# Taking attention's keys in passes, with a banked start and tail: two transformer layers on one core

## The chip, the cores and the metric

The kernel runs on one core of a Trainium2 chip. The metric is the device time of one execution in microseconds (us), as the median of several. The core's engines run side by side and wait for each other by semaphores: TensorE (PE, matrix products into the eight banks of PSUM), VectorE (DVE), ScalarE (ACT, functions such as exp and tanh), GpSimd (POOL) and SyncE (SP, which starts transfers here). Each engine takes its own instructions in program order.

## The reference

Two identical rounds of an attention layer and a feed-forward layer (FFN) on x, 2048 rows of 512 numbers in bf16:

```python
x = x + _A_ref(_layernorm(x), A_wqkv, A_wo)     # attention, 32 heads of 16
x = x + _B_ref(_layernorm(x), B_w1, B_w2)       # FFN: silu(x @ w1) @ w2, w1 512x1792
x = x + _A_ref(_layernorm(x), A_wqkv, A_wo)     # the same weights again
x = x + _B_ref(_layernorm(x), B_w1, B_w2)

def _A_ref(x, wqkv, wo):
    qkv = (x @ wqkv).reshape(B, S, 3, H, Dh).transpose(2, 0, 3, 1, 4)
    q, k, v = qkv[0], qkv[1], qkv[2]
    scores = einsum("bhqd,bhkd->bhqk", q, k) * Dh ** -0.5
    p = softmax(scores)                          # over all 2048 keys
    o = einsum("bhqk,bhkd->bhqd", p, v)
    return o.transpose(0, 2, 1, 3).reshape(B, S, D) @ wo
```

With heads of only 16, the exponentials (2 x 32 x 2048 x 2048) weigh more than the products.

## The kernel before

Rows are taken in four chunks of 512 queries; L is the round (0 or 1), qc the chunk, g one of four groups of eight heads, par the half of a group (heads are packed four at a time, j, into rows of 32 with the other half masked to zero), kt one of 16 tiles of 128 keys. One *block* is the scores of one head against one key tile, 128 keys x 512 queries. All blocks of both rounds form one stream. A *step* takes three blocks (even steps) or two (odd steps) through one exp on ScalarE; on even steps one more block may take its exp on VectorE, in integer and fp16 arithmetic (`emit_d`, `step_d`).

```python
blocks = list(stream())          # for L, qc, g, par, kt (16), j (4)
while pos < len(blocks):
    n = 3 - len(steps) % 2
    a = blocks[pos : pos + n]                                       # ScalarE's
    pos += n
    d = blocks[pos : pos + 1] if n == 3 and pos % 64 < D_LAST else []   # VectorE's, D_LAST = 54
    pos += len(d)
    steps.append((a, d))
```

The rest of the work (layernorm, Q, K, V, output projection, FFN) is written as generators, and waits in a queue, `bg`. Each step of the stream lets the queue go one piece further (`pump`: two matmuls, or a layernorm part); a number yielded is a number of steps to rest. What the stream needs at once is forced (`ensure`), in one burst.

```python
for t, (a_blks, d_blks) in enumerate(steps):
    for L, qc, g, par, kt, j in a_blks + d_blks:
        ...
        if j == 0 and kt % 4 == 0:
            if kt == 0 and par == 0:
                bg.ensure(("q", L, qc, g))
            if qc == 0:
                c = kt // 4
                bg.ensure(("k", L, c, g))          # keys and values of chunk c of x
                bg.ensure(("v", L, c))
    s_ps = ps_s.tile([P, size, 512], FP32, ...)    # 3 banks or 2, one buffer each
    for i, blk in enumerate(a_blks):
        score(blk, s_ps[:, i, :])
    for blk in d_blks:
        emit_d(blk)
    ...                                            # P*V of steps t-3, t-2 on odd steps: emit_pv
    run_d()
    if not run_urgent(t):                          # a finished group's output: group_out
        bg.pump()
    p_tiles[t] = ppool.tile([P, size, 512], BF16, ...)
    nc.scalar.activation(p_tiles[t], s_ps, ACT.Exp, bias=shift, scale=SCALE)
# after the stream: the rest of the queue, one piece after the other
```

All background work shares one PSUM bank, `ps_m` (bufs=1). The two pieces that matter most:

```python
def layernorm_T(c, dst):
    ...                                            # bn_stats, bn_aggr of four tiles; rstd on GpSimd
    yield 2
    for i in range(4):
        xns.append(tensor_scalar(x_sb[:, 4 * c + i, :], mv, rstd))     # DVE, all four
    yield 0
    for i in range(0, 4, 2):
        t_ps = ps_m.tile(...)
        ...                                        # 8 transposes, then a DVE copy into dst

def ffn(L, c, emit):
    yield from layernorm_T(c, fT)
    for ft in range(FT):                           # 14
        h_ps = ps_m.tile(...)
        ...                                        # 4 matmuls
        nc.scalar.activation(t_sb, h_ps, ACT.Tanh, scale=0.5)
        nc.vector.scalar_tensor_tensor(hT[:, ft, :], t_sb, 1.0, h_ps, add, mult)
        yield 1
    for tq in range(4):
        y_ps = ps_m.tile(...)
        ...                                        # 14 matmuls, then x_sb += 0.5 * y_ps; round 1: store
```

`proj_v` begins with a GpSimd memset of its V tile. At a group's end `group_out` transposes the result (through `ps_m` too) and divides by the sum of the exponentials, which a column of ones in V brings along.

Of the kernel before, what the change touches and what calls it, by code (L numbers as in the profile page):

```python
# [10 lines left out]
ACT = mybir.ActivationFunctionType  # L11
# [7 lines left out]


class Background:

    def __init__(self):
        self.queue = deque()
        self.done = set()
        self.wait = 0
        self.inside = False

# [3 lines left out]
    def step(self):  # L32
        label, gen = self.queue[0]
        try:
            gap = next(gen)
            self.inside = gap is None
            return gap or 0
        except StopIteration:
            self.queue.popleft()
            self.done.add(label)  # L40
            return -1

    def pump(self):
        if self.wait > 0:
            self.wait -= 1
            return
        while self.queue:
            gap = self.step()
            if gap >= 0:
                self.wait = gap  # L50
                return
# [5 lines left out]
    def ensure(self, label):  # L57
        while label not in self.done:
            self.step()
            self.wait = 0  # L60
# [3 lines left out]
def kernel(  # L64
# [31 lines left out]
    D_LAST = 54  # L96
# [6 lines left out]
    qpool = ctx.enter_context(tc.tile_pool(name="qpool", bufs=6))  # L103
    xtpool = ctx.enter_context(tc.tile_pool(name="xtpool", bufs=4))
    ftpool = ctx.enter_context(tc.tile_pool(name="ftpool", bufs=1))
    xnpool = ctx.enter_context(tc.tile_pool(name="xnpool", bufs=4))
# [3 lines left out]
    apool = ctx.enter_context(tc.tile_pool(name="apool", bufs=2))  # L110
# [3 lines left out]
    ps_s = ctx.enter_context(tc.tile_pool(name="ps_s", bufs=1, space=bass.MemoryType.PSUM))  # L114
    ps_o = ctx.enter_context(tc.tile_pool(name="ps_o", bufs=1, space=bass.MemoryType.PSUM))
    ps_m = ctx.enter_context(tc.tile_pool(name="ps_m", bufs=1, space=bass.MemoryType.PSUM))
# [15 lines left out]
    x_sb = xpool.tile([P, NKT, D], BF16, name="x_sb")  # L132
    w_qkv = wpool.tile([P, CT, 3 * D], BF16, name="w_qkv")
    wo_sb = wpool.tile([P, CT, D], BF16, name="wo_sb")
    w1_sb = wpool.tile([P, CT, F], BF16, name="w1_sb")
    w2_sb = wpool.tile([P, FT, D], BF16, name="w2_sb")

    def load_x(c):
        nc.sync.dma_start(
            x_sb[:, 4 * c : 4 * c + 4, :],  # L140
            xf[512 * c : 512 * (c + 1), :].rearrange("(tt p) d -> p tt d", p=P),
        )

    load_x(0)
    nc.sync.dma_start(w_qkv[:], A_wqkv.rearrange("(ct p) f -> p ct f", p=P))
    for c in range(1, NC):
        load_x(c)
    nc.sync.dma_start(wo_sb[:], A_wo.rearrange("(ct p) e -> p ct e", p=P))
    nc.sync.dma_start(w1_sb[:], B_w1.rearrange("(ct p) f -> p ct f", p=P))
    nc.sync.dma_start(w2_sb[:], B_w2.rearrange("(ft p) e -> p ft e", p=P))  # L150

# [5 lines left out]
    attn = {}  # L157

    def layernorm_T(c, dst):
        mv = small.tile([P, 4, 2], FP32, name="mv", tag="mv")  # L160
        for i in range(4):
            st = small.tile([P, 6], FP32, name="st", tag="st")
            nc.vector.bn_stats(st[:], x_sb[:, 4 * c + i, :])  # L163
            nc.vector.bn_aggr(mv[:, i, :], st[:])
            if i == 1:
                yield 0
        rstd = small.tile([P, 4, 1], FP32, name="rstd", tag="rstd")
        nc.gpsimd.tensor_scalar_add(rstd[:], mv[:, :, 1:2], float(EPS))
        nc.gpsimd.tensor_tensor(out=rstd[:], in0=rstd[:], in1=half[:], op=ALU.pow)
        yield 2  # L170
        xns = []
        for i in range(4):
            xn = xnpool.tile([P, D], BF16, name="xn", tag="xn")
            nc.vector.tensor_scalar(  # L174
                out=xn[:],
                in0=x_sb[:, 4 * c + i, :],
                scalar1=mv[:, i, 0:1],
                scalar2=rstd[:, i, :],
                op0=ALU.subtract,
                op1=ALU.mult,  # L180
            )
            xns.append(xn)
        yield 0
        for i in range(0, 4, 2):
            t_ps = ps_m.tile([P, CT, 2, P], BF16, name="t_ps", tag="m")
            for u in range(2):
                for ct in range(CT):
                    nc.tensor.transpose(  # L188
                        t_ps[:, ct, u, :], xns[i + u][:, ct * P : (ct + 1) * P], ident[:, :]
                    )  # L190
                if u == 0:
                    yield None
            nc.vector.tensor_copy(
                out=dst[:, :, i * P : (i + 2) * P].rearrange("p c (u q) -> p c u q", u=2),
                in_=t_ps[:],
            )
            yield 0
# [4 lines left out]

    def proj_k(L, c, g):
        if g == 0:
            KT[L, c] = kpool.tile([P, NG, 512], BF16, name="KT", tag="KT")
        k_ps = ps_m.tile([P, 512], FP32, name="k_ps", tag="m")
        for ct in range(CT):
            nc.tensor.matmul(
                k_ps[:],
                lhsT=w_qkv[:, ct, D + P * g : D + P * (g + 1)],  # L210
                rhs=xnT[L, c][:, ct, :],
                start=(ct == 0),
# [441 lines left out]
```

The softmax here doesn't subtract the row's maximum and nothing guards it: scores larger than these inputs give would overflow.

## Time and profile before

| | us |
|---|---|
| median of 4 runs (2156.25 to 2164.57) | 2163.52 |
| span of the profiled execution | 2160.7 |
| ACT: exp of 3 blocks, 704 of them, mean of one | 1.591 |
| ACT: exp of 2 blocks, 704, mean of one | 1.167 |
| ACT: tanh of the FFN, 112, mean of one | 0.709 |
| DVE: first part of its exp (d_y), 576, mean of one | 0.687 |
| PE: scores (s_ps), 3520, mean of one | 0.423 |
| PE: second FFN matmul (f_ps), mean of one | 0.413 |

Lines of the profile name the engine, the source line, the operation and its tiles (out<-in), with shapes as partitions x elements. The means include overlap: the next instruction on an engine may start before the one ahead of it has ended. A square bracket at the end of a line of the timeline gives how long the engine was idle before it and what released it. In the row of slices each digit is the busy share of a fortieth of the span in tenths.

### The profile page before, as it was taken

What the parts mean: (1) busy time and instruction counts of PE and PEld (TensorE: products, weight loads), DVE (VectorE), ACT (ScalarE), POOL (GpSimd) and SP (SyncE); (2) the same over time, 40 slices, a digit from 0 to 9 for tenths busy, and PEclk for the clock granted to TensorE, in tenths of its full rate; (3) what the DMA queues carried; (4) which work ended last, traced back from release to release, by engine and by line L of the source; (5) the groups of instructions that cost most, each with busy time, mean ns of one, the idle gap of its engine ahead of it and who ended that gap; (6) DMA issues with size and microseconds to landing.
All of it is one profiled execution on the core that took longest, in us unless ns stands there. A gap on an engine that the chain in (4) does not pass through costs nothing.

```text
span 2160.7 us, 27606 instructions
## 1 busy us (share of the span) xinstructions
PE 1644.5 (76%) x10684; PEld 484.7 (22%) x10816; DVE 1468.6 (68%) x2923; ACT 1795.1 (83%) x1521; POOL 37.2 (2%) x47
## 2 busy tenths in 40 slices
PE   4687777787778887788657777778877787878756
PEld 1222112222222222222222222222222222222122
DVE  4577668768877787778524666767767776876641
ACT  1289999999999999989405999999998999999931
POOL 1100000000000000000000000000000000000000
PEclk9698779999999998999766787889988998999756
DMA  3000000000000000000000000000000000000000
GB/s 146 0 1 1 1 1 1 1 1 1 1 1 1 1 1 1 1 1 1 0 0 1 1 1 1 1 1 3 8 1 1 1 11 1 1 1 8 3 1 10
DMA packets 7939, 11.72 MB, mean 5 GB/s; under 512 B 384, under 2 KB 6784, under 8 KB 7808
## 3 DMA queue, kind: packets, MB, share of 16 engines
q1 hardware_dynamic: 7808, 9.96, 1.3%
q8 instruction: 84, 1.38, 0.3%
q14 instruction: 47, 0.39, 0.1%
HBM read 7.86 MB, written 2.10 MB: 5 GB/s over the span
## 4 chain that ended last, share of the span: by engine, by line
ACT 32%; PE 26%; issue 23%; DVE 18%; another core or an unknown queue 0%; POOL 0%; DMA 0%; ACTq 0%; POOLq 0%; DVEq 0%
ACT p_sb L603 29%; PE o_ps L434 8%; PE s_ps L526 6%; PE h_ps L320 3%; DVE d_y L459 3%; PE f_ps L345 3%; ACT t_sb L331 3%; DVE st L163 2%; PE v_ps L245 2%; PE t_ps L188 1%; DVE d_r L497 1%; DVE d_r L502 1%; DVE d_r L498 1%; DVE hT L332 1%; DVE d_r L479 1%
## 5 line engine op out<-in xcount | busy, mean ns | idle before, releaser
L603 ACT ACTIVATE p_sb<-s_ps,shift 128x1536 bf16<-128x1536 f32 (+1 forms) x1408 | 1757.8, 1379 | 229.5 <-PE d_ps L526 180.4
L526 PE MATMUL s_ps<-QT,KT 32*128 32x512 bf16 x3520 | 597.2, 423 | 303.2 <-ACT p_sb L603 281.4
L459 DVE TENSOR_SCALAR d_y<-d_ps 128x512 uint16<-128x512 f32 x576 | 395.7, 687 | 352.0 <-PE d_ps L526 349.3
L434 PE MATMUL o_ps<-p_sb,VA 128*32 128x512 bf16 x3520 | 631.9, 429 | 0.4 <-ACT p_sb L603 0.4
L526 PEld LDWEIGHTS <-KT 32*128 32x128 bf16 x4096 | 180.6, 92 | 846.0 <-issue 823.5
L526 PE MATMUL d_ps<-QT,KT 32*128 32x512 bf16 x576 | 245.9, 427 | 7.1 <-DVE d_y L459 7.1
L434 PEld LDWEIGHTS <-VA 128*32 128x32 bf16 x4672 | 146.5, 98 | 294.2 <-issue 240.5
L502 DVE TENSOR_TENSOR d_r<-d_r,d_y 128x1024 f16<-128x1024 f16 (+1 forms) x320 | 201.5, 630 | 1.7
L497 DVE TENSOR_TENSOR d_r<-d_r 128x1024 f16<-128x1024 f16 (+1 forms) x320 | 201.6, 630 | 0.0
L320 PE MATMUL h_ps<-fT,w_sb 128*128 128x512 bf16 x404 | 147.9, 460 | 41.1 <-DVE hT L332 37.4
L331 ACT ACTIVATE t_sb<-h_ps 128x512 f32<-128x512 f32 x112 | 79.4, 709 | 113.9 <-PE h_ps L320 108.1
L332 DVE SCALAR_TENSOR_TENSOR hT<-t_sb,h_ps 128x512 bf16<-128x512 f32 x112 | 76.6, 684 | 104.2 <-ACT t_sb L331 103.4
L345 PE MATMUL f_ps<-w_sb,hT 128*128 128x512 bf16 x415 | 131.5, 413 | 13.5 <-DVE attn L270 4.8
L498 DVE TENSOR_SCALAR d_r<-d_r 128x1024 f16<-128x1024 f16 (+1 forms) x320 | 133.5, 417 | 11.1
L434 PE MATMUL o_ps<-d_r,VA 128*32 128x512 f16 x576 | 137.7, 429 | 2.5 <-DVE d_r L502 2.5
L434 PE MATMUL o_ps<-d_e,VA 128*32 128x512 f16 x576 | 139.0, 432 | 0.0
L479 DVE TENSOR_SCALAR d_r<-d_y 128x512 int32<-128x512 int32 (+1 forms) x320 | 129.1, 403 | 8.8
L487 DVE TENSOR_SCALAR d_e<-d_y 128x512 int32<-128x512 int32 (+1 forms) x320 | 125.9, 393 | 0.0
L188 PE MATMUL t_ps<-ident,xn 128*128 128x128 bf16 x256 | 34.7, 298 | 56.7 <-DVE xn L174 49.0
L443 DVE CAST oT<-o_ps 128x512 bf16<-128x512 f32 x64 | 44.0, 688 | 47.1 <-PE o_ps L434 47.1
L320 PEld LDWEIGHTS <-w_sb 128*128 128x128 bf16 x448 | 35.4, 108 | 134.2 <-issue 129.5
L245 PE MATMUL v_ps<-w_qkv,xnT 128*128 128x512 bf16 x122 | 50.5, 539 | 17.2 <-DVE VA L254 12.1
(40 smaller groups left out, 608.0 us busy)
## 6 DMA issues: line engine op xcount, KB each, us to landing
w_sb<-in_B_w_dram SPq DMA_DIRECT2D x2, 1792.0 KB, 13.0
x_sb<-in_A_x_dram SPq DMA_DIRECT2D x4, 512.0 KB, 8.4
out_dram<-x_sb SPq DMA_DIRECT2D x16, 128.0 KB, 1.7
w_qkv<-in_A_wqkv_dram SPq DMA_DIRECT2D x1, 1536.0 KB, 7.1
wo_sb<-in_A_wo_dram SPq DMA_DIRECT2D x1, 512.0 KB, 8.6
```

Source lines behind the costliest of these rows:

```text
L320: nc.tensor.matmul(h_ps[:], lhsT=w1_sb[:, ct, ft * P : (ft + 1) * P], rhs=fT[:, ct, :], start=(ct == 0), stop=(ct == CT - 1),)
L331: nc.scalar.activation(t_sb[:], h_ps[:], ACT.Tanh, scale=0.5)
L345: nc.tensor.matmul(y_ps[:], lhsT=hT[:, ft, tq * P : (tq + 1) * P], rhs=w2_sb[:, ft, :], start=(ft == 0), stop=(ft == FT - 1),)
L434: nc.tensor.matmul(o_tiles[key][32 * j : 32 * j + 32, :], lhsT=lhsT, rhs=rhs, start=(n[j] == 1), stop=(n[j] == o_total[key][j]),)
L459: nc.vector.tensor_scalar(out=pr["y"][:, len(pr["blks"]), :], in0=s_ps[:], scalar1=float(1024 * SCALE * math.log2(math.e)), scalar2=float( ...
L479: nc.vector.tensor_scalar(out=rf.bitcast(I32), in0=y.bitcast(I32), scalar1=0x03FF03FF, scalar2=0x3C003C00, op0=ALU.bitwise_and, op1=ALU.bi ...
L487: nc.vector.tensor_scalar(out=ef.bitcast(I32), in0=y.bitcast(I32), scalar1=0x7C007C00, scalar2=None, op0=ALU.bitwise_and,)
L497: nc.vector.tensor_tensor(out=rf, in0=rf, in1=rf, op=ALU.mult)
L498: nc.vector.tensor_scalar(out=rf, in0=rf, scalar1=EXP_C, scalar2=EXP_A, op0=ALU.mult, op1=ALU.add)
L502: nc.vector.tensor_tensor(out=rf, in0=rf, in1=y.bitcast(FP16), op=ALU.mult)
L526: nc.tensor.matmul(out, lhsT=KT[L, kt // 4][r, g, (kt % 4) * P : (kt % 4 + 1) * P], rhs=QT[L, qc, g][r, par, :], start=True, stop=True,)
L603: nc.scalar.activation(p_tiles[t][:, 0:n, :].rearrange("p a b -> p (a b)"), s_ps[:, 0:n, :].rearrange("p a b -> p (a b)"), ACT.Exp, bias=s ...
```

## The change

It does not touch what is computed, only its order. The stream is to begin as soon as the first chunk of x is ready, to cross from round 0 to round 1 without waiting for the last chunk's FFN, and the end is to be shorter. Partial sums over the keys of one pass are kept in SBUF, and added up by the transposing matmuls of `group_out`. Cut to its core:

```diff
-    D_LAST = 54
+    D_LEFT = 10
+    PASSES = {(0, 0): [range(0, 4), range(4, 8), range(8, NKT)], (1, 0): [range(0, 12), range(12, NKT)]}
...
-    xnpool = ctx.enter_context(tc.tile_pool(name="xnpool", bufs=4))
+    xnpool = ctx.enter_context(tc.tile_pool(name="xnpool", bufs=2))
+    papool = ctx.enter_context(tc.tile_pool(name="papool", bufs=8))     # partial sums
...
-    load_x(0)
-    nc.sync.dma_start(w_qkv[:], A_wqkv.rearrange("(ct p) f -> p ct f", p=P))
+    for i in range(0, 4, 2):
+        nc.sync.dma_start(x_sb[:, i : i + 2, :], ...)
+    for i in (1, 0, 2):                                                  # K, Q, V
+        nc.sync.dma_start(w_qkv[:, :, D * i : D * (i + 1)], wq[:, :, D * i : D * (i + 1)])
...
     def layernorm_T(c, dst):
-        ... four xn, then all transposes
+        for i in range(0, 4, 2):
+            xns = [ln_apply(c, k, mv[:, k, :], rstd[:, k, :]) for k in (i, i + 1)]
+            yield gap(0)
+            yield from ln_transpose(i, xns, dst)
...
     def group_out(L, qc, g, par, oT):
         for tq in range(4):
-            nc.tensor.transpose(att, oT[...], ident)
+            for i, o in enumerate(oT):                                   # 1 to 3 partial sums
+                nc.tensor.matmul(att, lhsT=o[...], rhs=ident, start=(i == 0), stop=(i == len(oT) - 1))
...
-        d = blocks[pos : pos + 1] if n == 3 and pos % 64 < D_LAST else []
+        d = blocks[pos : pos + 1] if n == 3 and pos < len(blocks) else []
+        if d and d[0][7] < D_LEFT:                                       # blocks left in this run
+            d = []
...
-    def ready_d():           # both blocks of a VectorE pair at once, four steps after its last
+    def ready_d(t):          # each block seven steps after it was issued
...
     def run_urgent(t):
         group_out(...)
+        bg.at = t + 2        # the queue rests for a step
...
+        with psum_whole("a"):                                            # 8 banks, before the stream
+            w_ps = bank("warm")
+            for i in range(56):
+                nc.tensor.matmul(w_ps[:, 0:P], lhsT=ident[:], rhs=ident[:], start=True, stop=True)
+            new_v(0, 0)                                                  # the memset
+            ... layernorm, K, Q, V of chunk 0
+        stream_psum.enter_context(psum_stream())                         # then the pools of before
...
             if not run_urgent(t):
-                bg.pump()
+                if not bg.queue and t % 2 == 0:
+                    warm(2)                                              # 2 matmuls whose result is not used
+                bg.pump(t, pe=True)
...
-        while bg.queue:
-            bg.step()
+        stream_psum.close()
+        with psum_whole("z"):                                            # 8 banks again
+            tail(1, NC - 1)                                              # output projection and FFN of the last chunk
```

In `tail` the FFN's two products are interleaved: after the first product of tile k come the four second products of tile k - 3, into four banks of their own. `ensure` of V now stands at the block's P*V and not at its scores. A rest after a background piece is at most `Pace.gap`: 0 in chunk (0,0) and in the first pass of (1,0), and 1 elsewhere.

## The prediction

> **What bounds the kernel now.** I read the page's busy times and slices first, then the windows, then ScalarE's timeline in the gaps, then the tail, then the small stalls.
>
> ```profile
> PE 1644.5 (76%) x10684; PEld 484.7 (22%) x10816; DVE 1468.6 (68%) x2923; ACT 1795.1 (83%) x1521; POOL 37.2 (2%) x47
> ...
> ACT  1289999999999999989405999999998999999931
> ```
>
> ScalarE (ACT) is busiest, but its row has three holes: the first slices, the middle, and the end. A slice is 54 us. Windows cut at these borders (columns: window, length, then busy us and count of PE, weight loads, DVE, ACT, POOL, then clock, DMA share, GB/s):
>
> ```profile
> 0.00:111.00 111.00, 63.19 (x245) 21.63 (x249) 58.42 (x117) 21.72 (x18) 13.97 (x19) 0.81 0.19 71
> 111.00:320.00 209.00, 166.44 (x1083) 44.25 (x1090) 144.55 (x290) 196.69 (x160) 0.00 (x0) 0.81 0.00 1
> 320.00:1028.00 708.00, 564.54 (x4001) 169.60 (x4062) 547.14 (x1092) 670.96 (x571) 13.75 (x15) 0.94 0.00 1
> ...
> 1048.00:1156.00 108.00, 62.38 (x189) 22.16 (x193) 33.94 (x60) 9.67 (x16) 4.45 (x5) 0.60 0.00 0
> ...
> 2068.00:2161.00 93.00, 52.98 (x165) 19.45 (x165) 23.74 (x41) 9.00 (x15) 1.27 (x2) 0.59 0.02 6
> ```
>
> In 320:1028 ACT is 95% busy: there it sets the pace. In the holes no engine is full; they are chains. ScalarE's own timeline (start, us, ..., idle before and its releaser) shows the first hole:
>
> ```profile
> 31.58 6.41 ACT L603 ACTIVATE p_sb<-s_ps,shift 128x1536 bf16<-128x1536 f32 x5 [29.31 <-PE d_ps L526]
> 57.51 1.11 ACT L603 ACTIVATE p_sb<-s_ps,shift 128x1024 bf16<-128x1024 f32 x1 [19.51 <-PE s_ps L526]
> 59.02 4.98 ACT L603 ACTIVATE p_sb<-s_ps,shift 128x1536 bf16<-128x1536 f32 x4 [0.40 <-PE d_ps L526]
> 83.03 2.55 ACT L603 ACTIVATE p_sb<-s_ps,shift 128x1536 bf16<-128x1536 f32 x2 [19.03 <-PE d_ps L526]
> ...
> 110.71 1.54 ACT L603 ACTIVATE p_sb<-s_ps,shift 128x1536 bf16<-128x1536 f32 x1 [19.68 <-PE d_ps L526]
> ```
>
> First exp at 31.58, then three waits of 19 to 20 us, one for each further chunk of x (its layernorm, K and V done in one burst because the stream needs keys of all 16 tiles at once): 58.2 us. The same rows give the floor: four exps take 4.98, two take 2.55, so one pair (3 + 2 blocks) costs 2.43 us. The middle hole is one such burst: an exp ends at 1048.65, the next starts at 1155.34, 106.7 us, with the rest of layer 0's last FFN and layer 1's last K/V between. The tail, in the timeline, is a ring through one PSUM bank:
>
> ```profile
> 2096.36 0.60 ACT L331 ACTIVATE t_sb<-h_ps 128x512 f32<-128x512 f32 x1 [27.71 <-PE h_ps L320]
> 2096.99 0.69 DVE L332 SCALAR_TENSOR_TENSOR hT<-t_sb,h_ps 128x512 bf16<-128x512 f32 x1 [2.58 <-ACT t_sb L331]
> 2097.73 1.87 PE L320 MATMUL h_ps<-fT,w_sb 128*128 128x512 bf16 x4 [1.41 <-DVE hT L332]
> 2099.63 0.60 ACT L331 ACTIVATE t_sb<-h_ps 128x512 f32<-128x512 f32 x1 [2.68 <-PE h_ps L320]
> ...
> 2150.29 3.18 PE L345 MATMUL f_ps<-w_sb,hT 128*128 128x512 bf16 x14 [0.78 <-DVE x_sb L354]
> ```
>
> One FFN tile takes 2099.63 - 2096.36 = 3.27 us, 14 of them 45.8. From the last exp's end (2068.64) to the end is 92 us: 2.9 to the attention tile, 14.2 output projection, 8.8 layernorm and transposes, 45.8, 17.9 second matmul, 2.5 store.
>
> The stream itself ran from 31.58 to 2068.64 = 2037.1 us. 704 pairs x 2.43 = 1711, plus 84 tanh between exps at 0.48 each (a tanh started at 424.00, its exp at 424.48) = 40. So 2037.1 - 1751 - 58.2 - 106.7 = 121 us are small stalls, some 15 in each of eight chunks. Lining the exps' start times up with the step that each belongs to, three kinds stand out: layernorm steps (1.2 to 3.9 us each, 5 to 9 per chunk in layer 0), the start of the FFN's second matmul (about 3), and stretches without background work, where steps with nine P*V matmuls lose 0.8:
>
> ```profile
> 247.66 1.48 PE L434 MATMUL o_ps<-p_sb,VA 128*32 128x512 bf16 x3
> ...
> 424.97 0.80 PE L434 MATMUL o_ps<-p_sb,VA 128*32 128x512 bf16 x3
> ```
>
> The same three matmuls, after the same six others, take 1.48 at 247 us and 0.80 at 424 us.
>
> [...] 512-column matmuls lasted 0.60 to 0.63 us in the holes and the idle stretches, 0.38 to 0.39 in the dense ones, and the rows above are the two states. [...] in the trace the DVE line 498 took 1.68 us at 495.99 instead of 0.36 while a GpSimd memset ran from 495.44 for 2.10. The change keeps those memsets in the stream.
>
> **The change part by part.** (a) *Passes.* In chunk (0,0) the keys are taken in three passes (4, 4, 8 tiles over all heads), in (1,0) in two (12, 4). I listed the changed kernel's PE instructions and assigned them to steps. Before, steps 4, 9 and 15 carry 36 background matmuls each, step 719 carries 184 and the last step 164. After, no step of the stream carries more than 12 (a three-part transpose), only the tail has 164. So 58.2 goes, and 106.7 goes except that its 14 tanh now stand between exps (6.7, counted below). The price: the DVE exp skips the last ten blocks of each run, and runs are shorter, so DVE blocks fall from 576 to 537 and ACT blocks rise from 3520 to 3559, 1424 steps instead of 1408. New floor: 711.5 pairs x 2.43 = 1729, plus 98 tanh x 0.48 = 47: 1776. The 24 extra copies of partial sums (0.69 each) lie on DVE, which then has fewer blocks to do.
>
> (b) *Start.* Loads of x in halves and w_qkv in thirds, eight PSUM banks, 56 small matmuls to warm PE, and the V memset before the layernorm. Before: statistics from 4.6, first scores 30.9. After: four tiles of statistics at 0.80 until 7.8, two normalised tiles 0.96, transposes and copy 1.5 (10.3), the second pair again 2.4 (12.7), K 0.9, Q 0.9, V 16 x 0.22 = 3.5 on PE without the 0.78 waits for a bank (18), last copy 0.7, scores 0.5: first exp near 20 (22 if PE is still cold). Saves about 11.
>
> (c) *Tail.* Eight banks, FFN matmuls interleaved with a lag of three tiles. 2.9 stays; projection and statistics overlap on DVE (2 transposes-and-copy, 4 adds and 4 statistics at about 0.8: some 9 instead of 17); rstd, normalise, transposes about 5; then 112 matmuls at 3.18/14 = 0.227: 25.4 instead of 61; four output adds 2.8, store 2.5, about 3 to fill and drain. Sum about 51. Saves 41.
>
> (d) *Small stalls.* Normalising two tiles instead of four, a step of rest after each group's output (the FFN matmul no longer stands behind it), one DVE-exp block's P*V in every odd step instead of two in every other, and two warming matmuls on even steps when the queue is empty (224 in the stream, 112 steps). I take the idle-stretch losses to go (11 + 14 in the two first chunks, some 10 in the last three: 35), the FFN start (3 x 6 = 18), half of the layernorm's (about 18): 121 - 71 = 50. Against it, 229 steps now carry background work without gaps; some 5 us: 55.
>
> Sum: 20 + 1776 + 55 + 51 = 1902; I say 1905.
>
> **Rivals.** *The dense passes make PE or DVE the bound.* In 229 steps nearly every step has two full-size matmuls, all through one bank, so PE can stand behind a DVE copy and scores come late. For: waits on that bank are already in the profile. Against: before, the second FFN matmul ran at seven such steps of eight and held 1.23 us a step; matmuls per step in the passes (7.1, 7.3) are below 7.7 of chunk (0,1). If they ran at 1.42 like the cold stretches: +46, 1950.
>
> *The warming does nothing, and fresh bank waits replace old stalls.* Warm tiles take the same single bank as a group's output, so PE may wait there for DVE. Then 121 stays: about 1970. A cold tail adds 112 x 0.2 = 22 more.
>
> *More goes than I count.* With hardly any small stalls left (15) and 18 + 46 at the ends: 1855.
>
> *The holes come back elsewhere*, as one late burst where a pass outruns its K or V. The instruction order speaks against it; it would cost 20 a time.
>
> **Range and chances.** The two large terms (58 and 100) are removed by order and nearly certain; tail and start are chains whose parts are measured; the stalls are the soft term, 15 to 120. That gives 1870 to 1950 for eight in ten. Slower than -2% (2120) would need all holes to come back: faster 0.97, same 0.02, slower 0.01.
>
> **What would show it.** First exp near 20; no ACT wait over 5 us in the stream; ACT row 9 from the first slice to the last but one; last exp end to span end near 51; in the tail, h and f matmuls at 0.22; matmuls of 0.39 instead of 0.60 in stretches without background; stream time minus 1776 near 55. Wrong would be: a wait of 10 us or more in the middle, a pace above 1.35 in the passes, or a tail above 70.

## The result, and the profile after

| | us |
|---|---|
| kernel before, median of 13 runs (2156.25 to 2169.53) | 2164.50 |
| changed kernel, median of 8 runs (1971.22 to 1983.39) | 1975.66 |
| ratio to the kernel before, 95% interval | 0.9128 (0.9114 to 0.9143) |
| span of the profiled execution | 1981.4 |

The kernel is faster by 8.7%, some 189 us. The prediction, 1905, was 71 us too low, and its range (1870 to 1950) does not hold the result.

The page of the changed kernel, busy times and ScalarE's row of slices (a slice is now 49.5 us):

```profile
PE 1567.8 (79%) x10999; PEld 472.5 (24%) x11169; DVE 1410.6 (71%) x2843; ACT 1814.4 (92%) x1537; POOL 37.6 (2%) x51
...
ACT  5899999998999998998979989999999999989992
```

The holes in the row are gone: no slice between the first and the last is below 7. ACT went from 83% to 92%, at nearly the same busy time. ScalarE's timeline at the start (start, length, ..., idle before and its releaser):

```profile
21.37 4.98 ACT L720 ACTIVATE p_sb<-s_ps,shift 128x1536 bf16<-128x1536 f32 x4
27.66 2.61 ACT L720 ACTIVATE p_sb<-s_ps,shift 128x1536 bf16<-128x1536 f32 x2 [1.31 <-PE s_ps L491]
...
52.56 1.11 ACT L720 ACTIVATE p_sb<-s_ps,shift 128x1024 bf16<-128x1024 f32 x1 [3.09 <-PE s_ps L491]
```

The first exp starts at 21.37, and the three waits of 19 to 20 us have become one of 3.09 and ten of 0.22 to 1.79. The tail, in the timeline:

```profile
1957.75 0.60 ACT L349 ACTIVATE t_tail<-h_ps 128x512 f32<-128x512 f32 x1 [1.13 <-PE h_ps L248]
1959.48 0.60 ACT L349 ACTIVATE t_tail<-h_ps 128x512 f32<-128x512 f32 x1 [1.13 <-PE h_ps L248]
...
1973.09 3.62 PE L435 MATMUL f_ps<-w_sb,hT 128*128 128x512 bf16 x16
```

One FFN tile now takes 1959.48 - 1957.75 = 1.73 us with both its products in it, where the first product alone took 3.27; 16 matmuls take 3.62, or 0.226 each. The last exp ends at 1935.83: a tail of 45.5.

So the start, the three bursts, the crossing between the rounds and the tail came out as planned, and the missing 71 us lie inside the stream. It runs from 21.37 to 1935.83, 1914.5 us. Against the predicted floor of 1776 that leaves 138 us of small stalls where I had put 55. The table of waits shows them (engine and line that waited <- what released it: us, times, longest):

```profile
ACT p_sb L720 <- PE d_ps L491: 55.0, 77, 2.6
PE t_ps L223 <- DVE xn L209: 37.2, 23, 3.6
ACT p_sb L720 <- PE s_ps L491: 33.6, 47, 3.1
PE o_ps L528 <- DVE oT L546: 19.8, 29, 1.4
```

ScalarE waits for scores, 88.6 us in 124 waits, none above 3.1. Behind that, PE waits for DVE, most of all for the normalised tiles that it is to transpose.

**Where they lie.** As in the prediction, I lined each exp up with its step. A step's *stall* is the time from its exp's start to the next exp's, less 1.437 us for an exp of three blocks or 0.996 for two (the pair of 2.43) and 0.48 for a tanh between them. I then cut out the *layernorm windows*: from 1 us before a layernorm's first statistics to 4 us after its last transposing matmul. In the changed kernel there are 14, together 276 us. Stalls of the profiled execution in us:

| | before | after |
|---|---|---|
| chunks (0,1) to (0,3): in layernorm windows / outside | 27.0 / 18.1 | 30.7 / 24.7 |
| chunks (1,1) to (1,3): in layernorm windows / outside | 14.6 / 26.5 | 16.3 / 11.7 |
| chunks (0,0) and (1,0), the ones with passes | 190.9 | 52.2 |
| sum | 277.1 | 135.6 |

The chunks with passes fell as they should, though not to where I had put them. The six ordinary chunks together did not move: 86.2 before, 83.4 after. I had expected them to fall by more than half. In their layernorm windows the stalls even rose a little, from 41.6 to 47.0. Windows of the changed kernel (length, then busy us and count of PE, weight loads, DVE, ACT, POOL, then clock, DMA share, GB/s) show what is special there:

```profile
511.00:750.00 239.00, 186.58 (x1336) 53.69 (x1354) 181.62 (x364) 224.54 (x191) 4.44 (x5) 0.91 0.00 1
...
1477.00:1706.00 229.00, 179.58 (x1319) 52.71 (x1338) 170.19 (x342) 222.00 (x190) 1.25 (x2) 0.93 0.01 3
...
539.00:550.00 11.00, 5.28 (x47) 1.97 (x46) 10.33 (x24) 8.29 (x7) 1.27 (x2) 0.92 0.00 0
```

The first row is one whole chunk of round 0, the second one of round 1: DVE is busy 76% and 74%. The third is 11 us inside the first, around one layernorm: DVE is busy 94%, ACT only 75%, and PE 48%. Over all 14 windows DVE is busy 83%: 93 to 95% in the first layernorm of each chunk from (0,1) to (0,3), 84% in those of (1,1) to (1,3), but only 74 or 75% in the second layernorm of (0,1) to (0,3). The timeline around the 11 us:

```profile
541.61 0.66 DVE L198 BATCH_NORM_STATS2 st<-x_sb 128x6 f32<-128x512 bf16 x1
542.41 0.66 DVE L546 CAST oT<-o_ps 128x512 bf16<-128x512 f32 x1
543.12 0.59 PE L528 MATMUL o_ps<-p_sb,VA 128*32 128x512 bf16 x4 [1.36 <-DVE oT L546]
543.61 4.98 ACT L720 ACTIVATE p_sb<-s_ps,shift 128x1536 bf16<-128x1536 f32 x4 [1.30 <-PE o_ps L528]
...
548.85 0.73 DVE L209 TENSOR_SCALAR xn<-x_sb,mv,rstd 128x512 bf16<-128x512 bf16 x2
549.32 0.61 PE L223 MATMUL t_ps<-ident,xn 128*128 128x128 bf16 x4 [1.95 <-DVE xn L209]
550.58 5.15 ACT L720 ACTIVATE p_sb<-s_ps,shift 128x1536 bf16<-128x1536 f32 x4 [1.98 <-PE d_ps L491]
```

The copy that frees the bank of a group's result (oT) stands on DVE behind two statistics; PE waits for it 1.36 us and ScalarE 1.30. Then the normalised tiles come late, PE waits for them 1.95 us with the next scores behind the transposes, and ScalarE 1.98.

The second layernorms of (0,1) to (0,3) stall most, 5.8 to 6.5 us each against 4.1 to 4.5 in the first, though DVE is not busy throughout. In one of them DVE is busy 5.67 of the 6 us from 680.5, while the statistics run. Then it waits for GpSimd, and its two normalised tiles take 2.34 us beside a memset on GpSimd, against 0.73 above:

```profile
687.72 1.97 POOL L280 MEMSET VA<- 128x2240 bf16 x1
687.80 2.34 DVE L209 TENSOR_SCALAR xn<-x_sb,mv,rstd 128x512 bf16<-128x512 bf16 x2 [1.46 <-POOL rstd L204]
```

### The profile page after: what moved, and what is told of

It is laid out like the page before. It is cut to its first block, busy times and chain, and to the rows that moved or that the text cites. A ratio compares the mean times of both kernels' runs of the same rounds, so it can differ in the third digit from the quotient of the medians.

```text
span 1981.4 us, 28267 instructions
## 1 busy us (share of the span) xinstructions
PE 1567.8 (79%) x10999; PEld 472.5 (24%) x11169; DVE 1410.6 (71%) x2843; ACT 1814.4 (92%) x1537; POOL 37.6 (2%) x51
## 4 chain that ended last, share of the span: by engine, by line
ACT 34%; PE 25%; issue 23%; DVE 17%; POOL 0%; ACTq 0%; DVEq 0%; POOLq 0%
ACT p_sb L720 32%; PE o_ps L528 7%; PE s_ps L491 7%; DVE d_y L558 3%; PE h_ps L248 3%; ACT t_sb L349 3%; DVE st L198 2%; DVE d_r L579 2%; DVE d_r L597 1%; PE f_ps L382 1%; PE t_ps L223 1%; DVE d_e L587 1%; DVE d_r L598 1%; DVE QT L273 1%; DVE xn L209 1%
## 5 line engine op out<-in xcount | busy, mean ns | idle before, releaser
L558 DVE TENSOR_SCALAR d_y<-d_ps 128x512 uint16<-128x512 f32 x537 | 368.6, 686 | 297.3 <-PE d_ps L491 296.1
L528 PE MATMUL o_ps<-p_sb,VA 128*32 128x512 bf16 x3559 | 543.4, 416 | 25.1 <-DVE oT L546 19.8
L528 PE MATMUL o_ps<-d_e,VA 128*32 128x512 f16 x537 | 224.6, 419 | 0.0
L491 PE MATMUL d_ps<-QT,KT 32*128 32x512 bf16 x537 | 221.1, 412 | 2.5 <-DVE d_y L558 2.4
L528 PE MATMUL o_ps<-d_r,VA 128*32 128x512 f16 x537 | 220.4, 410 | 0.0
L528 PEld LDWEIGHTS <-VA 128*32 128x32 bf16 x4633 | 114.3, 96 | 249.1 <-issue 228.0
L382 PE MATMUL f_ps<-w_sb,hT 128*128 128x512 bf16 x357 | 112.1, 388 | 7.1 <-DVE x_sb L355 2.1
L404 PE MATMUL warm<-w_sb,ident 128*128 128x512 bf16 x207 | 67.7, 399 | 2.4 <-DVE attn L311 0.9
L349 ACT ACTIVATE t_sb<-h_ps 128x512 f32<-128x512 f32 x98 | 62.8, 641 | 4.0 <-PE h_ps L248 4.0
L223 PE MATMUL t_ps<-ident,xn 128*128 128x128 bf16 x256 | 34.1, 280 | 37.2 <-DVE xn L209 37.2
L273 DVE TENSOR_SCALAR QT<-q_ps,mask 128x512 bf16<-128x512 f32 x64 | 44.9, 744 | 17.5 <-PE q_ps L248 17.5
```

The source lines that it names most:

```text
L382: nc.tensor.matmul(y_ps, lhsT=hT[:, ft, tq * P : (tq + 1) * P], rhs=w2_sb[:, ft, :], start=(ft == 0), stop=(ft == FT - 1),)
L491: nc.tensor.matmul(out, lhsT=KT[L, kt // 4][r, g, (kt % 4) * P : (kt % 4 + 1) * P], rhs=QT[L, qc, g][r, par, :], start=True, stop=True,)
L528: nc.tensor.matmul(o_tiles[key][32 * j : 32 * j + 32, :], lhsT=lhsT, rhs=rhs, start=(n[j] == 1), stop=(n[j] == o_total[key][j]),)
L558: nc.vector.tensor_scalar(out=pr["y"][:, len(pr["blks"]), :], in0=s_ps[:], scalar1=float(1024 * SCALE * math.log2(math.e)), scalar2=float( ...
```

## The experiments

**What was to be told apart.** A: in a layernorm DVE has more to do than fits beside its share of the exps, so that every us of DVE work there is a us of the time. B: PE stands behind DVE only because the order is unlucky; another order or a rest hides the wait. C: PE is slow there (around the layernorm shown above the granted clock was 1.00 from 539 to 545 us, 0.81 to 550 and 0.59 to 556). D: the *phase* of the runs, that is at which step (even or odd) and block of the step a run of 64 blocks begins. Before, every run began with an even step; the passes shift it, to the second block of an even step in chunks (0,1) to (0,3), and of an odd step in (1,1) to (1,3). Unless said otherwise, "the ordinary chunks" are these six, and stalls are given as in windows / outside (changed kernel: 47.0 / 36.4). Stall sums come from one execution each; the profiled one of the changed kernel was the slowest of its eight (1983.39), so differences below some 10 us are read from the ratios. A ratio is always to the kernel before, and 0.001 is 2.2 us.

### Parts of the change

**One pass (e4).**

```diff
-    PASSES = {(0, 0): [range(0, 4), range(4, 8), range(8, NKT)], (1, 0): [range(0, 12), range(12, NKT)]}
+    PASSES = {}
```

> The changed kernel with a single pass over all keys in every chunk, so that K and V of later chunks of x are forced in bursts again; start, tail, pacing and warming stay. Both theories: about 58 us of waits come back in chunk (0,0) and about 100 at round 1's beginning, less 18 for 39 fewer ACT blocks. Theory phase: as every run is again 22 whole steps, chunks (0,1) to (0,3) fall to about 230 although all their work is the same; time near 2095. Theory work: they stay at 238-240; time near 2120.

2098.86 us, 0.970 (0.968 to 0.9719), so the passes are worth 124 us net. Stalls of (0,0) and (1,0) are 85.6 and 97.3 instead of 21.4 and 30.8, and the floor is 19 us lower (1759.7 against 1778.8). The runs now start with an even step as before, and the ordinary chunks still have 46.1 / 42.3: their stalls are not the passes' doing. The time came near the 2095 of theory phase, but not in its way: the stalls of (0,1) to (0,3) are 53.2, against 55.4 in the changed kernel.

**No warming in the stream (e3).**

```diff
-                if not bg.queue and t % 2 == 0:
-                    warm(2)
```

> The changed kernel without the 224 warming matmuls in the stream. As predicted at first they keep PE fast where no background work is left: without them round 1's last three chunks should lose some 3 to 8 us each and matmuls of 0.60 us should be back there, time 1985 to 2000. Theory phase puts the difference between round 0 and round 1 elsewhere and expects round 0's chunks to stay at 238-240 and the time to move by less than 12 us. Theory work, with warming as the reason: round 1's last three chunks rise to 238, time near 2000.

2002.96 us, 0.9259 (0.9242 to 0.9275): warming is worth 28 us. The window of (1,0)'s second pass, which has no background work, in the changed kernel and then without warming:

```profile
1186.00:1246.00 60.00, 48.87 (x357) 16.84 (x359) 31.81 (x77) 58.97 (x49) 0.00 (x0) 1.00 0.00 1
```

```profile
1186.00:1260.00 74.00, 62.53 (x361) 16.21 (x363) 35.56 (x85) 67.22 (x55) 0.00 (x0) 0.68 0.00 1
```

The granted clock is 1.00 and 0.68, and ScalarE is busy 98% and 91%. (1,1) to (1,3) lost less than expected: 7 us together of some 23 more in all.

**VectorE's P*V in pairs again (e7).**

```diff
-            pr = pairs[0]
-            i = len(pr["blks"]) - len(pr["at"])
+            pr = pairs.popleft()
...
-            mms += pv_block(pr["blks"][i], ...)
-            pr["at"].pop(0)
-            if not pr["at"]:
-                pairs.popleft()
+            for i, blk in enumerate(pr["blks"]):
+                mms += pv_block(blk, ...)
```

> The changed kernel with the P*V of both blocks of a DVE pair in one odd step again (9 and 5 matmuls in turn instead of 7 and 7), as before the change. My prediction had the smoothing and the warming together remove 35 us, and the warming alone is now worth 27 (2003 against 1976): so 5 to 10 us slower, about 1984. Rival: with PE fast, nine matmuls fit into a step as well as seven, and nothing changes within 3 us.

1978.59 us, 0.9168 (0.9153 to 0.9183), 9 us slower than the changed kernel's ratio. As expected.

**No rest after a group's output (e8).**

```diff
         group_out(...)
-        bg.at = t + 2
```

> The changed kernel without the rest of a step after a group's output. As predicted the rest keeps the next matmul from standing behind the division on DVE in the one bank: without it 10 to 18 us slower, 1986 to 1994, and PE waits on attn grow from about 2 to 10 us or more. Rival: the rests only make the queue later [...]; without them the time falls by 5 to 10.

1992.36 us, 0.9228 (0.9196 to 0.9259): the rest is worth some 22 us, more than the 10 to 18 expected. The table of waits:

```profile
PE h_ps L248 <- DVE attn L311: 8.4, 11, 1.1
PE f_ps L382 <- DVE attn L311: 8.2, 12, 0.8
PE a_ps L324 <- DVE attn L311: 5.3, 7, 1.1
```

Without the rest, the next piece's matmul stands behind DVE's division of the group's output (attn), in the one bank they share. Outside the layernorm windows the ordinary chunks lose 67.1 instead of 36.4.

### The phase of the runs

**Every run starts with an even step (e1).**

```diff
-        n = 3 - len(steps) % 2
+        n = min(3 - len(steps) % 2, blocks[pos][7] + 1)
+        if len(steps) % 2 == 0 and n == blocks[pos][7] + 1:
+            n -= 1
...
-        d = blocks[pos : pos + 1] if n == 3 and pos < len(blocks) else []
+        d = blocks[pos : pos + 1] if n == 3 and len(steps) % 2 == 0 and pos < len(blocks) else []
```

> The changed kernel, with every run of blocks (one pass of one half group) starting on an even step; 24 steps hold one block for it. Theory phase: in the changed kernel a run ends inside a step from the third pass of chunk (0,0) on, so a piece of the next run's P*V comes one step after the last of the old run and waits for the DVE copy of the one o_ps bank; aligned, PE's waits on the oT copy (19.8 us in the profile) go to about 0, chunks (0,1) to (0,3) fall from 238-240 us to about 230, the first pass of (1,0) from 198 by about 10, and the time from 1976 to about 1935. Theory work: round 0's chunks are slow because of their layernorm, K and V pieces and because nothing warms PE there; then they stay at 238 and the time at 1976 within 5 us.

1996.19 us, 0.9226 (0.9211 to 0.924), slower by 21. The wait of o_ps for oT, 19.8 us in the changed kernel, did vanish, but the stalls of (0,1) to (0,3) stayed at 54.5, against 55.4. As the cause of the layernorm stalls, phase falls.

**Only the later chunks of round 1 shifted (e2).**

```diff
-        n = 3 - len(steps) % 2
+        n = {894: 2, 895: 1}.get(len(steps), 3 - len(steps) % 2)
```

> The changed kernel, with one step added just before chunk (1,1), so that the runs of chunks (1,1) to (1,3) start as those of (0,1) to (0,3) do, on the second block of an even step; nothing else differs. Theory phase: these three chunks rise from 229-231 us to about 237 each, the time by about 22 to 1998. Theory work: they stay, the time is the same within 3 us.

1989.26 us, 0.9185 (0.9153 to 0.9217), slower by 12, where D expected 22. In (1,1) to (1,3), which now begin their runs as (0,1) to (0,3) do, the stalls in windows stayed (16.3 and 13.5), those outside rose from 11.7 to 24.4.

So phase is an effect of its own, of some 12 us for three chunks, outside the layernorms. Among the 13 kernels that change neither the rests nor the warming, the stalls outside the windows of (1,1) to (1,3) are 11.7 to 13.1 in the six whose runs all begin there on an odd step's second block (the changed kernel, e6, e7, e10, e15, e17), and 21.0 to 28.1 in the seven where most or all do not (e1, e2, e4, e13, e14, e16, e18). Only e2 was made for it; the rest is read afterwards, from kernels that differ in other things too. No run gave round 0 the good phase throughout, so what it would bring there was not tried.

### Order, rest and clock in the layernorm

**A further step between normalising and transposing (e5).**

```diff
-            yield gap(0)
+            yield (False, True, 1)
```

> The changed kernel with one more step between normalising two tiles and transposing them in every layernorm. Theory late DVE: the layernorm stalls (about 9 us per round 0 chunk, 4 per round 1 chunk) come from PE standing in order behind the normalised tiles, which DVE delivers late (37.2 us of PE waits on xn); with a step more PE's waits on xn fall below 12 us and the time falls by 15 to 30, to about 1950. Theory DVE load: the layernorm's DVE work displaces the DVE exp whatever the order, so the stalls only move to scores of DVE blocks (waits of PE on d_y grow) and the time stays within 5 us.

1968.75 us, 0.9122 (0.9098 to 0.9146), the same as the changed kernel. The table of waits:

```profile
PE t_ps L223 <- DVE xn L209: 10.7, 14, 2.5
PE d_ps L491 <- DVE d_y L558: 9.6, 11, 2.0
```

PE's wait for the normalised tiles fell from 37.2 to 10.7, as B wanted, and nothing came of it: the ordinary chunks have 30.2 / 51.6. The wait that I had read as the cause only showed where a late DVE was felt first. Some of it now stands as a wait for DVE's exp (9.6; 2.4 in the changed kernel).

**PE kept warm through the layernorm (e9).**

```diff
+                warm(2)                    # after the second tile's statistics
...
-        yield (False, False, 2)
+        for _ in range(3):
+            warm(2)
+            yield NEXT_NO_PE
...
+        warm(4)                            # between normalising and transposing
```

> The changed kernel with warming matmuls (two at each statistics and resting step, four at each normalising step) inside every layernorm of the stream, where PE otherwise waits. Theory slow clock: [...] it is then the half clock, not the late tiles, that costs most of the 5 us per layernorm, since the slow stretch outlasts them; kept fast, the stalls halve: ratio from 0.913 to about 0.903, and score matmuls of 0.6 us fall from 171 steps to under 100. Theory DVE load: scores are late because DVE is; the stalls stay, ratio 0.913 within 0.003, or worse as the warming holds up scores.

1976.04 us, 0.9113 (0.9069 to 0.9158), the same. The mean clock rose from 0.916 to 0.943 and the steps with slow scores (above 0.5 us) fell from 171 to 115, but the stalls stayed at 137.8. PE's wait for the normalised tiles fell from 37.2 to 8.4, and the ordinary chunks have 39.5 / 50.3: what the windows gained came back outside them. The test is not clean, because the warming matmuls themselves waited 22.8 us for DVE to empty their bank (9.2, 7.2 and 6.4 for three kinds of tile). So C finds no support here, and e13, below, loses most of the layernorms' stalls with a lower clock in the window shown there (0.80 against 0.92).

**Warming on every rest (e11), and both kinds of warming with a small memset (e12).**

```diff
+        bg.cool = t + 1                    # after a group's output
...
+                if bg.queue and not bg.inside and bg.cool < t < bg.at and t % 2 == 0:
+                    warm(2)
```

> The changed kernel with two warming matmuls also on even steps in which the queue has work but rests (not right after a group's output, where the bank is still being read). Theory slow clock: round 0's chunks lose about 18 us each against 9 in round 1 because nothing warms PE there; they fall by 4 to 8 us each, ratio near 0.905. Theory DVE load: round 0's chunks stay within 2 us, ratio 0.913 or more.

> All three that may help together: warming inside layernorms, warming on rests, and the small memset. If slow clock is right, the best version so far: ratio near 0.895. If DVE load is right: near 0.911, the small memset's gain alone.

2018.72 us, 0.9319 (0.9274 to 0.9364), and 2005.85 us, 0.9247 (0.9205 to 0.9289): slower by 41 and 26 than the changed kernel's ratio. The table of waits of the first:

```profile
PE warm L405 <- DVE hT L351: 36.3, 41, 1.2
PE warm L405 <- DVE QT L274: 17.3, 11, 2.3
```

The warming matmuls take the one background bank, so PE waits for DVE to empty it, with scores behind. This is the rival of fresh bank waits: true where warming stands beside other work, and hardly in the change, which warms only while the queue is empty (the largest entry of this kind in its table of waits is 2.9 us, eight waits together).

### The work on VectorE

**Statistics of one tile for four (e10).** This kernel leaves out three of the four statistics in each of the 14 layernorms of the stream, and normalises all four tiles by the first one's, so its output is another. On the page DVE's busy time falls from 1410.6 to 1377.7, 33 us or 2.35 a layernorm, and GpSimd's from 37.6 to 31.3; PE's work stays. The page of this run:

```profile
PE 1553.4 (80%) x10999; PEld 467.4 (24%) x11169; DVE 1377.7 (71%) x2759; ACT 1811.7 (93%) x1537; POOL 31.3 (2%) x51
```

```diff
-        mv, rstd = yield from ln_stats(c, range(4))
...
+        nc.vector.bn_stats(st[:], x_sb[:, 4 * c, :])
+        nc.vector.bn_aggr(mv[:, 0, :], st[:])
...
-            xns = [ln_apply(c, k, mv[:, k, :], rstd[:, k, :]) for k in (i, i + 1)]
+            xns = [ln_apply(c, k, mv[:, 0, :], rstd[:, 0, :]) for k in (i, i + 1)]
```

> The changed kernel with the statistics of one tile in four only (the other three tiles are normalised with the first one's mean and variance, so the output is another): 2.5 us of DVE work left out per layernorm of the stream, 14 of them. Theory DVE load: each layernorm's stall falls by 2 to 2.5 us, about 30 in all: ratio near 0.900. Theory slow clock: the clock still falls while PE waits for the normalised tiles; less than 10 us, ratio 0.909 or more.

1943.17 us, 0.8968 (0.8931 to 0.9005): 32 us less by the medians, 35 by the ratios. The table of waits:

```profile
ACT p_sb L727 <- PE d_ps L498: 38.3, 69, 1.4
PE t_ps L223 <- DVE xn L209: 20.5, 22, 2.5
ACT p_sb L727 <- PE s_ps L498: 18.7, 32, 1.8
```

Stalls fell from 135.6 to 98.3. The ordinary chunks have 27.3 / 36.6: nine of the 14 layernorms are theirs, 21 us of the work left out, and they gained 19.7 in the windows and gave nothing back outside. Each us of DVE work left out took about one off the time. The three kinds of layernorm gained alike: 6.4 us in the three first ones of (0,1) to (0,3), 6.6 in the three second ones, 6.9 in round 1's. GpSimd's shorter part accounts for little, as DVE's waits for it fell only from 5.9 to 3.0 us. This is A, and of the runs the one that shows it cleanest.

**No exp on DVE around a layernorm (e13).** In eight steps around each of the 14 layernorms (`QUIET` lists the steps) ScalarE takes all blocks. Nothing is left out.

```diff
-        if d and d[0][7] < D_LEFT:
+        at = len(steps) - begin.setdefault(a[0][0:2], len(steps))
+        if d and (d[0][7] < D_LEFT or any(w - 7 <= at < w + 1 for w in QUIET[a[0][0:2]])):
```

> The changed kernel with no exp on DVE in the eight steps around each of the 14 layernorms of the stream; 34 blocks go to ACT instead, which raises the floor by 34 x 0.44 = 15 us, and relieves DVE of some 1.3 us a block just where it is short. Theory DVE load: the layernorm's 5 us of stall go nearly all (14 x 4.5 = 63 at most, 40 allowing for what other waits keep); net 25 to 45 us faster, ratio 0.893 to 0.902. If the stalls come from anything that does not depend on DVE's load (the order of waits, PE's clock): the stalls stay and the floor's 15 us come on top, ratio near 0.920.

1958.66 us, 0.9047 (0.9017 to 0.9078). 34 blocks moved to ScalarE and the floor rose by 16.7, yet the time fell by 17, less than the 25 to 45 expected. The window of the same layernorm as above:

```profile
529.00:540.00 11.00, 8.55 (x59) 2.83 (x57) 6.57 (x16) 10.62 (x10) 1.27 (x2) 0.80 0.01 1
```

DVE is busy 60% instead of 94%, ScalarE 97% instead of 75%, and this at a lower clock (0.80 against 0.92). The ordinary chunks have 8.6 / 48.5. A moved block also spares PE one matmul of three, so this run alone would not single out DVE; e10 does. The rise outside is round 1's phase (26.2, from 11.7), which the moved blocks shift.

**The quiet steps with a small memset (e14), the memset alone (e6).** The GpSimd memset of a V tile writes only the columns that V leaves open.

```diff
-        nc.gpsimd.memset(VA[L, c][:], 1.0)
+        nc.gpsimd.memset(VA[L, c][:, :, 0 : 17 * H].rearrange(...)[:, :, :, DH:17], 1.0)
+        nc.gpsimd.memset(VA[L, c][:, :, 17 * H : VW], 1.0)
```

> The changed kernel with the GpSimd memset of a V tile limited to the column of ones of each head and the padding at the end (about a twelfth of the elements). [...] the memset of 2 us holds up the DVE exp's fast operations in the layernorm before K and V in round 0, as DVE lines of 1.7 instead of 0.4 us show; without it chunks (0,1) to (0,3) lose 2 to 3 us less each, with (0,0) and (1,0) 10 to 15 us in all, time near 1963. [...]

> The same with the small memset as well. Theory DVE load: GpSimd's memset lengthens DVE work in the layernorms of round 0; with DVE relieved there, the memset matters less than the 3 us it cost alone: ratio equal to the run without it, or 0.001 to 0.003 less. The candidate for a version that beats both kernels.

Alone 1967.22 us, 0.9114 (0.9093 to 0.9136); with the quiet steps 1956.85 us, 0.903 (0.8993 to 0.9067). Each is 3 to 4 us better than its partner without it, inside the intervals; the 10 to 15 us expected of the memset did not come, though on GpSimd it fell from 1.97 us to two instructions of 0.65 and 0.45 (medians in e6).

**Twelve quiet steps instead of eight (e16).**

```diff
-... any(w - 7 <= at < w + 1 for w in QUIET[a[0][0:2]])
+... any(w - 9 <= at < w + 3 for w in QUIET[a[0][0:2]])
```

> As the first of this call, with twelve steps around each layernorm instead of eight: 48 blocks go to ACT, the floor rises by 21 us. Theory DVE load: a little of the layernorm's stall that eight steps leave goes too, but about as much as the floor gains: within 8 us of the eight-step run.

1983.38 us, 0.9147 (0.9117 to 0.9177), 22 slower than with eight, which I had not expected. The windows are nearly empty of stalls (4.0) but the ordinary chunks lose 59.9 outside them, and the floor is another 7 higher. This kernel's runs begin in many different phases; whether that is the reason was not separated.

**No exp on DVE in the first pass of (1,0) (e15).** 50 blocks move to ScalarE, floor +24.

```diff
-        if d and d[0][7] < D_LEFT:
+        if d and (d[0][7] < D_LEFT or a[0][0:3] == (1, 0, 0)):
```

> The changed kernel with no exp on DVE in the first pass of (1,0), the densest stretch of background work; 50 blocks go to ACT, the floor rises by 22 us. What is open is whether that pass's 30 us of stalls are DVE load as well. If so, they fall to 10 or less, and the time stays within 5 us of the changed kernel's, ratio 0.913. If they come from PE (two matmuls in every step at half clock, or standing behind the one bank's copies), they stay at 25 or more and the ratio is near 0.923.

1989.86 us, 0.9182 (0.9152 to 0.9212). That pass's stalls fell from 29.9 to 12.6, 17 us for 24 of floor: the load is a cause there too, but moving all of it costs more than it frees. Whether it is DVE's load or PE's this run does not tell, as 50 matmuls go with the exps. The start of that pass in the changed kernel, in the timeline and in a window:

```profile
1001.90 1.03 PE L248 MATMUL y_ps<-wo_sb,aT 128*128 128x512 bf16 x2
...
1003.59 1.54 ACT L720 ACTIVATE p_sb<-s_ps,shift 128x1536 bf16<-128x1536 f32 x1 [1.37 <-PE d_ps L491]
```

```profile
1000.00:1016.00 16.00, 14.46 (x68) 3.12 (x69) 6.24 (x12) 9.81 (x9) 0.00 (x0) 0.51 0.00 0
```

Here it is not DVE (39% busy): PE is 90% busy at a granted clock of 0.51, with the output projection between the scores. Five steps that begin from 997.6 to 1013.1 lose 6.6 us.

**Quiet steps in round 0 and (1,0) only (e17), and also at the start of that pass (e18).** Both have the small memset.

```diff
+    QUIET = {(0, 0): [], (0, 1): [28, 131], (0, 2): [28, 131], (0, 3): [28, 131], (1, 0): [22, 102], (1, 1): [], ...}
```

> The changed kernel with the small memset, and no exp on DVE in the eight steps around a layernorm only in chunks (0,1) to (0,3) and the first pass of (1,0), where the quiet steps took 8 to 12 us of stalls each; round 1's last chunks and (0,0), where they took nothing, keep it. 20 blocks go to ACT, floor up by 9 us instead of 15. Theory DVE load: 4 to 8 us faster than with quiet steps everywhere, ratio 0.900 to 0.902. If the gain there came from a lucky shift of the steps, the ratio is back near 0.910.

> The same, and the first eight steps of (1,0) quiet as well (two blocks more to ACT): there the output projection's adds and copies come in every second step beside the DVE exp, and PE falls to half clock. Theory DVE load: the (1,0) first pass loses another 3 to 6 us of stalls, ratio 0.001 to 0.002 below the run beside it. Otherwise the two are the same or this one is a little slower.

e17: 1948.02 us, 0.9021 (0.8992 to 0.905), the lowest ratio of the kernels that leave nothing out, 1.2% below the changed one; its interval overlaps those of e13 and e14, so that the 4 to 8 us expected against them are not shown. 20 blocks moved, floor +9.9, stalls 91.8. The ordinary chunks have 21.2 / 33.1, and round 1 keeps its phase (11.7 outside). e18: 1960.18 us, 0.9061 (0.904 to 0.9082), slower than e17 where I expected a gain. (1,0) gained 3 us, but one step more shifted the phase of round 1, and its stalls outside windows went from 11.7 to 28.1.

## Why the prediction was wrong

- **(a) Passes: right in kind.** No wait above 3.1 us in the stream; e4 puts them at 124 us net. The floor came out at 1778.8 for 1776; four exps in a row take 4.98 us, as before.
- **(b) Start: right.** First exp at 21.37, for "near 20".
- **(c) Tail: right, and better.** 45.5 for 51; matmuls at 0.226 for 0.227.
- **(d) Small stalls: the step that failed.** The sum had 55, made of 50 and "some 5 us" for the dense steps. It measured 138 (135.6 against the exact floor). With 1.4 at the start and -5.5 at the tail, 1902 + 1.4 - 5.5 + 83 = 1981, the profiled span.

Of the three gains in (d), "35 for idle stretches" is borne out in kind (e3: 28, e7: 9), and so is the "18 for the FFN start" (e8: 22), though these price the parts inside the changed kernel and not what they took off the old one: outside the layernorm windows the ordinary chunks' stalls fell from 44.6 to 36.4, not by the 28 that (d) had there. **"Half of the layernorm's" is wrong.** I read a layernorm's stall as PE standing behind a batch of four normalised tiles, so that two would halve it. It is DVE's load: four statistics, four normalised tiles and two copies come to some 6 us (4 x 0.8 + 4 x 0.4 + 2 x 0.69 = 6.2), laid into pairs of 2.43 us of which a block's exp on DVE already takes about 1.76 (e13: 34 blocks fewer, busy time 1410.6 to 1350.8). Splitting moves no work off DVE, and the stalls in the windows stayed, 41.6 before and 47.0 after; no run puts back the batch of four alone. e5 and e9 moved the wait and the clock without gain; e10 took DVE work away and got it back one for one; e13 and e17 gave DVE's exps to ScalarE there and gained more than that costs.

**"Some 5 us" for the dense steps was mis-sized.** The 229 steps that (d) gave "some 5 us" kept 46.0 (11.8 and 4.3 in the first two passes of (0,0), 29.9 in the first of (1,0)). Of (1,0)'s 30.8 in both passes, 7.4 lie in layernorm windows and 6.6 in the start, where the granted clock was 0.50. e15 shows that 17 of the 29.9 go with the moved exps, and no run splits PE from DVE there.

By place, the 135.6 us are three parts. The layernorm windows of all chunks hold 64 (47.0, 10.0 in (0,0), 7.4 in (1,0)), where (d) left 18. Outside them the ordinary chunks hold 36, where 44.6 less 10 for idle stretches and 18 for the FFN start left 17. The rest of (0,0) and (1,0) holds 35, where 20 of the 55 remained. So of the missing 80 some 46 are the layernorms', for which the runs show the cause. Some 20 lie outside them in the ordinary chunks, most of it in round 0, and their cause stays open. Some 15 belong to the dense stretches, with the cause known in part.

A third thing was not in the prediction at all: the passes shift the phase of all later runs, for the better in round 1 (e2: undoing it costs 12 us). What it does in round 0, where the stalls outside the windows rose from 18.1 to 24.7, stays open.

**The rivals.** "Warming does nothing, fresh bank waits" came nearest in number, 1970, for the wrong reason: e3 contradicts the first half, and its bank waits appear only when forced (e11). "The dense passes make PE or DVE the bound" was right about these passes: it named 46 us, and their 229 steps kept 46.0. A pace above 1.35 us a step in the passes, named as a sign of being wrong, did show: 1.47 in the first of (0,0) and 1.49 in the first of (1,0). This rival did not have the ordinary chunks' layernorms. My arguments against it used matmuls per step, an average, and of DVE I counted nothing by stretch. The holes did not come back.

Two small slips in the prediction bear on nothing: its 711.5 pairs are 712, and line 498, for the shape it quotes (128x512), takes 0.29 us when no memset runs beside it, not 0.36.

The busiest engine changes within a chunk: over the chunk from 511 to 750 us ACT is busiest, 94% against DVE's 76%, and in the 11 us at its layernorm DVE, 94% against 75%.

## What to carry to other kernels

When one engine's steady stream is shared out to a second engine, look at that second engine in windows as short as a burst of its other work, not over the stage. Then take work off it there and see whether the time follows: here 33 us less of it saved 32 to 35, while a rest before the transposes moved PE's wait from 37.2 to 10.7 and saved nothing. A busy share alone does not rank the bursts, as the layernorms with 75% over 20 us stalled more than those with 95%. The cheap remedy in this kernel was to give the shared work back to the first engine for just those steps, and eight steps did better than twelve (e13, e16). And when a schedule's period is shifted by an edit far away, compare the phase in later stages before reading their times: here it was worth 12 us (e2), and e13, e14 and e18 had 13 to 16 us more stalls in round 1 where it differed.

## What was unexpected of the hardware

PE stayed at half clock while busy. From 980 to 991.9 the granted clock was 1.00, with PE busy 9.00 of 11.9 us; from 991.9 to 1015.8 it was 0.50, with PE busy 21.69 of 23.9. From 1000 to 1016 it was busy 14.46 of 16 us at 0.51, and two 512-column matmuls of the output projection took 1.03 us, as long as four full ones took in the tail at a granted clock of 1.00 (from 1957.55, 1.03). The prediction had found 0.60 to 0.63 us for such matmuls in holes and idle stretches, and 0.38 to 0.39 in dense ones; in this dense stretch the scores took 0.60 (median). It mixes score and P*V matmuls, which use a strip of 32 rows or columns (`32*128` and `128*32` in the trace), with full ones (`128*128`); whether that is why was not tried.

A higher mean clock brought nothing in two runs: 0.943 instead of 0.916 with the same time (e9), and the highest mean clock of the profiled executions, 0.951 in e12, belongs to one that is 26 us slower than the change.
